# Two more token tiles taken from a transposed copy of the input, their statistics spread through DRAM, in a gated linear-attention kernel on one core

## The chip, the cores and the metric

One Trainium2 chip, one of its cores. The metric is the time of one execution in device microseconds; a kernel's time is the median of its runs. Engines are named as in the profile: PE is TensorE (PEld its weight loads), DVE is VectorE, ACT is ScalarE, POOL is GpSimd, SP is SyncE, which issues most of the DMAs here.

## The reference

Everything is float32, with 2048 tokens of 640 features, 32 heads of 20 and a hidden width of 1536. A layer norm without weights is followed by a linear attention with a learned softmax feature map and by an MLP that gates it:

```python
xn = (x - mean(x)) / sqrt(var(x) + 1e-5)
q, k, v = split(xn @ wqkv)                       # 32 heads of 20 each
phi = lambda t: concat(softmax(t @ w_phi), softmax(-t @ w_phi))   # per head, 20 -> 40
kv, z = phi(k).T @ v, sum(phi(k))                # over all tokens, per head
s = ((phi(q) @ kv) / (phi(q) . z + 1e-6)) @ wo
g = silu(gelu(xn @ w1 + b1) @ w2 + b2)
out = x + s * g
```

The host hands the kernel x twice, as it is and transposed (xt), and regroups the weights; it does no arithmetic.

## The kernel before

**Precision.** A float32 matmul is made of three passes in fp32r: every operand is kept as a high and a low part, a "split" of one ACT copy (the high part) and one DVE subtraction (the low part), and PASSES multiplies high by high, high by low and low by high.

**Stages.** Phase 1 handles 16 token tiles of 128 tokens: layer norm, transposition of x, projections to k, v and q, feature maps, and the sums kv and z. Then come twelve units of the MLP, with the queries' normalisation beside them, and the output. In the stages that matter here the order of every engine's queue is the order of the code; nothing is scheduled. Before phase 1 the key weights are folded with w_phi on PE (fold_w, L179, 24 + 6 matmuls of L174), and ahead of that PE runs ten matmuls of a constant (L521).

**How a tile is normed and transposed.** There are two ways.

- Tiles 0 to 5: norm (L255) takes the tile from x with tokens on partitions; DVE makes its statistics (L230 to L232), POOL a power of -0.5 (L233), and DVE or ACT norms the tile (L246, L252). transpose_x (L357) has five PE transposes (L363) into PSUM, pA, and plain (L282) splits from there: ACT at L285, DVE at L287.
- Tiles 6 to 15, as pairs q = t // 2: load_xr (L262) loads the pair's columns from xt into a slab xr, with features on partitions. pair_stats (L330) makes the statistics of each tile from x as above; at the second tile SP writes them to DRAM (L337) and reads them back to all 128 partitions (L339, tile bc). pair_sub (L343) subtracts the means on POOL (L346, two instructions), pair_mul (L349) multiplies by the reciprocal deviations on DVE (L351), and pair_plain (L353) splits from xr.

plain writes to xp and, for odd tiles, also to a slab b that two pairs share (beside, L276). Every project of tile t reads them.

**The loop over tiles (L577 to L606)**, for t = 2 to 5. PE runs project(t, wk), for t = 3 and 5 kv_pair(t - 3), and value(t), in whose middle a lambda may put transpose_x(t + 2); for t = 4 and 5 fold_pair(t - 4) follows (two groups of L174, read by ACT at L196 and L199 and by DVE at L197 and L198). On the other engines feat1 (L386) reads the projected keys: DVE takes a maximum (L389), a difference (L392) and a minimum (L395), and POOL the reversed half (L396); feat2 is an exponential on ACT (L405); key_fin sums heads on DVE (L413, L445) and scales on POOL (L418). spill (L294) writes a pair's split columns to DRAM.

**PSUM.** project, transpose_x, fold and the first matmuls take their accumulators from one pool of three slots (pA, two banks each) that are used in turn. The slot is free again when its readers are done: L392 for keys, ACT's L434 for values, L285 and L287 for a transposed tile, the last reading of fold_pair at L198.

**Rows and slabs.** Tiles of x, raw weights and bc come from a pool of 11 rows, xr, e and the split weights from one of 23 slabs, each in turn.

Of the kernel before, what the change touches and what calls it, by code (L numbers as in the profile page):

```python
# [46 lines left out]
def hedgehog_gated_mlp_kernel(ctx: ExitStack, tc: tile.TileContext, x, xt_in, wqk, bd, wv, wo, w1, b1, w2, b2, out_t):  # L47
# [33 lines left out]
    def slab(dt, name, shape=(P, 2, D)):  # L81
        return slabs.tile(list(shape), dt, tag="S", name=name)

    def row(shape, dt, name):
        return rows.tile(shape, dt, tag="R", name=name)

    def bankA():
        return pools["A"].tile([P, 2, 512], F32, tag="A", name="pA")
# [136 lines left out]
    def stats(t, sm, mean, rstd):  # L225
        xt = xts.pop(t)
        st = sm[:, :12]
        for i in range(2):
            with tc.issue_after(last_feat[0].ins) if last_feat[0] is not None and not by_hand[0] else ExitStack():
                nc.vector.bn_stats(st[:, 6 * i:6 * i + 6], xt[:, i * HALF:(i + 1) * HALF])  # L230
        nc.vector.bn_aggr(sm[:, 12:14], st.rearrange("p (a b) -> p a b", a=2))
        nc.vector.tensor_scalar(rstd, sm[:, 13:14], LN_EPS, None, op0=OP.add)  # L232
        nc.gpsimd.tensor_tensor(rstd, rstd, mhalf[:], op=OP.pow)  # L233
        if mean is not None:
            nc.vector.tensor_copy(mean, sm[:, 12:13])
        return xt
# [3 lines left out]
    def norm_a(t):  # L240
        sm = small.tile([P, 16], F32, tag="st", name="st")
        nrm[t] = sm, stats(t, sm, None, sm[:, 14:15])

    def norm_b(t):
        sm, xt = nrm.pop(t)
        nc.vector.tensor_scalar(xt[:], xt[:], sm[:, 12:13], sm[:, 14:15], op0=OP.subtract, op1=OP.mult)  # L246
        xns[t] = xt
# [7 lines left out]
    def norm(t):  # L255
        norm_a(t)
        norm_b(t)
# [4 lines left out]
    def load_xr(q):  # L262
        h, p = divmod(q, SLOTS)
        xr = slab(F32, "xr", (P, KC, W2))[:]
        src = xt_in.rearrange("(k p) (h o q t) -> p k h o q t", p=P, h=NH, o=2, q=SLOTS)[:, :, h, :, p]
        nc.sync.dma_start(xr[:, :, :P], src[:, :, 0])
        nc.sync.dma_start(xr[:, :, P:], src[:, :, 1])
        xrs[q] = xr
# [13 lines left out]
    def plain(q, o, v):  # L282
        parts = [(xp[:, 0:5, :, at(q)], v)] if o == 0 else [(beside(q), v[:, 0:2]), (xp[:, 5:8, :, at(q)], v[:, 2:5])]
        for dst, src in parts:
            nc.scalar.activation(dst[:, :, 0, :], src, AF.Copy)  # L285
        for dst, src in parts:
            nc.vector.tensor_tensor(dst[:, :, 1, :], src, dst[:, :, 0, :].bitcast(F32), op=OP.subtract)  # L287

    def stat_x(q, o, k, a):
        if o == 0:  # L290
            return xp[:, k, a, at(q)]
        return beside(q)[:, k, a, :] if k < 2 else xp[:, k + 3, a, at(q)]
# [37 lines left out]
    def pair_stats(t):  # L330
        if t % 2 == 0:
            pst[0] = small.tile([P, 2, 2], F32, tag="pst", name="pst")
        sm = small.tile([P, 16], F32, tag="st", name="st")
        stats(t, sm, pst[0][:, t % 2, 0:1], pst[0][:, t % 2, 1:2])
        if t % 2:
            q = t // 2
            nc.sync.dma_start(st_dram[q].rearrange("i p s -> p i s"), pst[0][:])  # L337
            bc = row([P, W2, 2], F32, "bc")
            nc.sync.dma_start(bc[:].rearrange("p t s -> p (t s)"),  # L339
                              st_dram[q].rearrange("i p s -> (i p s)").partition_broadcast(P))  # L340
            pld[q] = bc

    def pair_sub(q):  # L343
        bc, xr = pld[q], xrs[q]
        for o in (slice(0, P), slice(P, W2)):
            nc.gpsimd.tensor_tensor(xr[:, :, o], xr[:, :, o], bc[:, None, o, 0].to_broadcast([P, KC, P]),  # L346
                                    op=OP.subtract)

    def pair_mul(q):  # L349
        bc, xr = pld.pop(q), xrs[q]  # L350
        nc.vector.tensor_tensor(xr, xr, bc[:, None, :, 1].to_broadcast([P, KC, W2]), op=OP.mult)  # L351

    def pair_plain(q):  # L353
        for o in range(2):
            plain(q, o, xrs[q][:, :, o * P:(o + 1) * P])

    def transpose_x(t):  # L357
        q, o = divmod(t, 2)
        xn = xns.pop(t)
        ps = bankA()  # L360
        flat = ps[:].rearrange("p a b -> p (a b)")
        for k in range(KC):
            nc.tensor.transpose(flat[:, k * P:(k + 1) * P], xn[:, k * P:(k + 1) * P], ident[:])  # L363
        plain(q, o, flat[:, :D].rearrange("p (k t) -> p k t", t=P))
# [3 lines left out]
    def project(t, ws, mid=None, at_k=3):  # L368
        q, o = divmod(t, 2)
        ps = bankA()  # L370
        n = 0
        for k in range(KC):
            if k == at_k and mid is not None:
                mid()
            for a, b in PASSES:
                for hf in range(2):
                    nc.tensor.matmul(ps[:, hf, :HALF], stat_x(q, o, k, a),  # L377
                                     ws[k][:, b, hf * HALF:(hf + 1) * HALF],
                                     start=n == 0, stop=n == 3 * KC - 1)
                n += 1  # L380
        return ps

    def heads(ps):
        return ps[:, :, :HALF].rearrange("p a (h d) -> p a h d", d=DH)

    def feat1(ps, later=None):  # L386
        p4 = heads(ps)
        mx = small.tile([P, 2, 16], F32, tag="mx", name="mx")
        nc.vector.tensor_reduce(mx[:], p4, axis=AX.X, op=OP.max)  # L389
        e = slab(F32, "e")[:]  # L390
        e5 = e.rearrange("p a (h s d) -> p a h s d", s=2, d=DH)
        nc.vector.tensor_tensor(e5[:, :, :, 0, :], p4, mx[:, :, :, None].to_broadcast([P, 2, 16, DH]),  # L392
                                op=OP.subtract)
        nr = small.tile([P, 2, 16], F32, tag="nr", name="nr")
        last_feat[0] = nc.vector.tensor_reduce(nr[:], e5[:, :, :, 0, :], axis=AX.X, op=OP.min)  # L395
        rest = lambda: nc.gpsimd.tensor_tensor(e5[:, :, :, 1, :], nr[:, :, :, None].to_broadcast([P, 2, 16, DH]),  # L396
                                               e5[:, :, :, 0, :], op=OP.subtract)
        if later is None:
            rest()
        else:  # L400
            later.append(rest)
        return e.rearrange("p a b -> p (a b)")
# [28 lines left out]
    def value(t, mid=None):  # L431
        ps = project(t, wv_s, mid)
        v, v3 = value_row()
        nc.scalar.activation(v3[:, :, :DH].rearrange("p (a h) d -> p a h d", a=2), heads(ps), AF.Copy)  # L434
        return v
# [12 lines left out]
    def key_fin(ef):  # L448
        scale_heads(ef, key_sums(ef))
        return ef  # L450
# [10 lines left out]
    vs, es, phis, xns, wk_s, wq_s = {}, {}, {}, {}, [], [None] * 4  # L461
# [54 lines left out]
    phase1 = ExitStack()  # L516
    phase1.enter_context(tc.manual_schedule(engines={mybir.EngineType.PE, mybir.EngineType.SP}))
    one = nc.const_aps.tensor(1.0, [P, P], F32)
    for pw in (bankA(),):
        for i in range(10):  # L520
            nc.tensor.matmul(pw[:, 0, :P], one, one, start=True, stop=True)  # L521
    startup = ExitStack()
    startup.enter_context(tc.manual_schedule())
# [35 lines left out]
    es[0] = feat1(pk)  # L559
    split_v(3)  # L560
    pk = project(1, wk_s, lambda: transpose_x(2))
    load_xr(3)
    x_in(8)
    x_in(9)
# [2 lines left out]
    feat2(es[0])  # L567
    norm(3)
    es[1] = feat1(pk)
    vs[0] = value(0)  # L570
    phis[0] = key_fin(es.pop(0))
    feat2(es[1])
    vs[1] = value(1, lambda: transpose_x(3))
    norm(4)
    phis[1] = key_fin(es.pop(1))
    vf = [v_forms(0), v_forms(1)]
    for t in range(2, 6):  # L577
        pk = project(t, wk_s)
        if t % 2:
            kv_pair(t - 3)  # L580
        es[t] = feat1(pk)
        if t == 4:
            next(vf[0])
        if t == 2:
            norm(5)
        if t == 3:
            pair_stats(6)
            pair_stats(7)
        if t > 3:
            pair_stats(t + 4)  # L590
        if t in (3, 4, 5):
            spill(t - 3)
        if t == 5:
            x_in(10)
        if t == 4:
            pair_sub(3)
            pair_mul(3)
        vs[t] = value(t, (lambda: transpose_x(t + 2)) if t < 4 else None)
        if t >= 4:
            fold_pair(t - 4)  # L600
        if t == 5:
            next(vf[0])
        feat2(es[t])
        if t == 4:
            pair_plain(3)
        phis[t] = key_fin(es.pop(t))  # L606
# [179 lines left out]
    for p in range(5, 8):  # L786
        t = 2 * p
# [18 lines left out]
        def rest(t=t, p=p):  # L806
            if p == 5:
                next(vb)
                next(vb, None)
            later.pop(0)()  # L810
            feat2(es[t])
            if p == 6:
                t_sums(7)
            if p == 7:
                next(qf)
# [542 lines left out]
```

## Time and profile before

| | us |
|---|---|
| median of 3 runs | 652.42 |
| the three runs | 652.40, 652.42, 653.68 |
| the profiled execution | 653.69 |
| its span, first to last instruction | 652.0 |
| PE busy | 646.4 (99%) |
| DVE busy | 486.9 (75%) |
| POOL busy | 400.7 (61%) |
| ACT busy | 237.9 (36%) |

A row of the time line begins with the start in us from the span's start and a duration in us, followed by engine, line, operation, output <- input, shapes and the number of instructions that were merged; in brackets stand the idle time before it and what ended that. A float32 matmul that isn't fp32r shows as two instructions. A row of the windows names a stretch, its length, the busy time and number of instructions of PE, PEld, DVE, ACT and POOL, the granted clock of PE, the share of the DMA engines and GB/s. A row of the waits says who waited at which line for whom: us in total, times, longest.

### The profile page before, as it was taken

What the parts mean: (1) busy time and instruction counts of PE and PEld (TensorE: products, weight loads), DVE (VectorE), ACT (ScalarE), POOL (GpSimd) and SP (SyncE); (2) the same over time, 40 slices, a digit from 0 to 9 for tenths busy, and PEclk for the clock granted to TensorE, in tenths of its full rate; (3) what the DMA queues carried; (4) which work ended last, traced back from release to release, by engine and by line L of the source; (5) the groups of instructions that cost most, each with busy time, mean ns of one, the idle gap of its engine ahead of it and who ended that gap; (6) DMA issues with size and microseconds to landing.
All of it is one profiled execution on the core that took longest, in us unless ns stands there. A gap on an engine that the chain in (4) does not pass through costs nothing. (4 is left out here: it accounts for less than half of the span.)

```text
span 652.0 us, 11424 instructions
## 1 busy us (share of the span) xinstructions
PE 646.4 (99%) x4396; PEld 561.4 (86%) x4396; DVE 486.9 (75%) x734; ACT 237.9 (36%) x345; POOL 400.7 (61%) x371
## 2 busy tenths in 40 slices
PE   9999999999999999999999999999999999999997
PEld 9999999999999998888888888888888886766866
DVE  5785976789887777587978977858889899853232
ACT  3522422334343348144343355742231524032130
POOL 2656466897967765857878775355462966343321
PEclk9999999999999999999999999999999999999999
DMA  9705377495312486355987998695969499999942
GB/s 349 281 2 146 116 279 219 102 308 150 124 42 62 143 280 245 121 188 183 306 236 258 244 414 286 123 336 195 177 232 249 65 269 206 317 266 260 301 135 80
DMA packets 164447, 135.15 MB, mean 207 GB/s; under 512 B 89394, under 2 KB 128562, under 8 KB 164010
## 3 DMA queue, kind: packets, MB, share of 16 engines
q1 hardware_dynamic: 161658, 122.84, 64.2%
q10 hardware_dynamic: 2736, 11.60, 4.8%
q8 instruction: 34, 0.56, 0.4%
q14 instruction: 19, 0.16, 0.1%
HBM read 86.03 MB, written 48.38 MB: 206 GB/s over the span
## 5 line engine op out<-in xcount | busy, mean ns | idle before, releaser
L944 PE MATMUL pB<-hs,w2s 128*128 128x512 f32 x720 | 165.8, 389 | 0.0
L944 PEld LDWEIGHTS pB<-hs,w2s 128*128 128x128 f32 x720 | 135.0, 188 | 28.8 <-DVE y L953 0.8
L915 PE MATMUL pB<-xp,w1s 128*128 128x512 f32 x324 | 81.3, 389 | 0.0
L915 PE MATMUL pB<-xd,w1s 128*128 128x512 f32 x324 | 79.3, 389 | 0.0
L1102 PE MATMUL pB<-oT,wo 128*128 128x512 f32 (+1 forms) x315 | 72.3, 381 | 0.0
L418 POOL TENSOR_TENSOR eq<-eq,rc 128x1280 f32<-128x1280 f32 x16 | 37.9, 2369 | 55.0 <-DVE rc L1006 36.7
L915 PEld LDWEIGHTS pB<-xd,w1s 128*128 128x128 f32 x324 | 60.8, 188 | 12.6
L915 PEld LDWEIGHTS pB<-xp,w1s 128*128 128x128 f32 x324 | 60.8, 188 | 12.6
L1102 PEld LDWEIGHTS pB<-oT,wo 128*128 128x128 f32 x315 | 57.2, 188 | 13.8 <-PE pB L1049 2.5
L953 DVE TENSOR_TENSOR y<-pB,y 128x512 f32<-128x512 f32 x100 | 63.1, 676 | 1.4 <-PE pB L944 1.4
L920 ACT ACTIVATE pB<-pB,b1t 128x512 f32<-128x512 f32 x48 | 31.8, 662 | 79.0 <-DVE pB L1183 29.2
L405 ACT ACTIVATE e<-e 128x1280 f32<-128x1280 f32 x32 | 40.7, 1273 | 53.0 <-POOL e L396 49.2
L377 PE MATMUL pA<-wk,xp 128*128 128x320 f32 x384 | 59.6, 310 | 0.0
L396 POOL TENSOR_TENSOR e<-nr,e 128x640 f32<-128x640 f32 x32 | 43.5, 1361 | 24.1 <-DVE nr L395 24.0
L377 PEld LDWEIGHTS pA<-wk,xp 128*128 128x128 f32 x384 | 56.9, 188 | 0.1
L418 POOL TENSOR_TENSOR e<-e,rc 128x1280 f32<-128x1280 f32 x16 | 37.8, 2368 | 24.0 <-DVE rc L445 24.0
L993 POOL TENSOR_TENSOR ez<-eq,zrep 128x1280 f32<-128x1280 f32 x16 | 47.3, 2957 | 2.6 <-DMA eq<-e_dram 2.6
L485 POOL TENSOR_TENSOR w1s<-raw,w1s 128x640 fp32r<-128x640 f32 (+1 forms) x18 | 27.3, 1517 | 28.9 <-ACT w1s L484 28.9
L377 PE MATMUL pA<-wv,xp 128*128 128x320 f32 x240 | 37.7, 311 | 0.0
L149 POOL TENSOR_TENSOR w2s<-raw,w2s 128x640 fp32r<-128x640 f32 x23 | 36.0, 1588 | 0.2 <-ACT w2s L147 0.2
L1105 POOL TENSOR_TENSOR xres<-gt,xres 128x256 f32<-128x256 f32 x20 | 14.3, 736 | 35.3 <-DVE gt L1104 35.3
L377 PEld LDWEIGHTS pA<-wv,xp 128*128 128x128 f32 x240 | 35.5, 188 | 0.1
(182 smaller groups left out, 1139.7 us busy)
## 6 DMA issues: line engine op xcount, KB each, us to landing
raw<-in_w_dram SPq DMA_DIRECT2D x42, 320.0 KB
e_dram<-e ACTq DMA_DIRECT2D x16, 640.0 KB
eq<-e_dram SPq DMA_DIRECT2D x16, 640.0 KB
phi_t<-eq SPq DMA_DIRECT2D x64, 160.0 KB
phT<-phi_t SPq DMA_DIRECT2D x20, 480.0 KB
xt<-in_x_dram SPq DMA_DIRECT2D x16, 320.0 KB
xres<-in_xt_dram SPq DMA_DIRECT2D x20, 256.0 KB
out_dram<-xres SPq DMA_DIRECT2D x18, 256.0 KB
```

The lines of the kernel that those rows point to most:

```text
L149: eng.tensor_tensor(sl[:, 1, :], raw, sl[:, 0, :].bitcast(F32), op=OP.subtract)
L377: nc.tensor.matmul(ps[:, hf, :HALF], stat_x(q, o, k, a), ws[k][:, b, hf * HALF:(hf + 1) * HALF], start=n == 0, stop=n == 3 * KC - 1)
L396: rest = lambda: nc.gpsimd.tensor_tensor(e5[:, :, :, 1, :], nr[:, :, :, None].to_broadcast([P, 2, 16, DH]), e5[:, :, :, 0, :], op=OP.subtract)
L405: nc.scalar.activation(ef, ef, AF.Exp)
L418: nc.gpsimd.tensor_tensor(e3, e3, rc[:, :, None].to_broadcast([P, 64, DH]), op=OP.mult)
L485: nc.gpsimd.tensor_tensor(sl[:, 1, :n], src, sl[:, 0, :n].bitcast(F32), op=OP.subtract)
L915: nc.tensor.matmul(bank[ch][:], tl[:, a, off + wo_:off + wo_ + P], mov(blk, b), start=new and n == 0, stop=n == len(mms) - 1, skip_group_c ...
L920: nc.scalar.activation(ps, ps, AF.Gelu_apprx_tanh, bias=b1t[:, f:f + 1])
L944: nc.tensor.matmul(ps[:], ws[i][:, b, d * P:(d + 1) * P], hs[o][i][:, a, :], start=i == n == 0, stop=(i, n) == (GF - 1, 2), skip_group_che ...
L953: nc.vector.tensor_tensor(y, ps[:], y, op=OP.add)
L993: nc.gpsimd.tensor_tensor(zv, ef, zf, op=OP.mult)
L1102: nc.tensor.matmul(ps[:, mv], w, o[:, mv], start=n == 0, stop=n == 15, skip_group_check=True)
```

## The change

Tiles 4 and 5 change from the first way to the second. load_xr(2) is added ahead of load_xr(3). norm(4), norm(5), transpose_x(4) and transpose_x(5) go; pair_stats(4) and pair_stats(5) stand behind feat1(1) and value(0), pair_sub(2) and pair_mul(2) take norm(5)'s place at t = 2, and pair_plain(2) stands at t = 3 ahead of pair_stats(6). The ten constant matmuls in one slot become nine in three.

```diff
-    for pw in (bankA(),):
-        for i in range(10):
+    for pw in (bankA(), bankA(), bankA()):
+        for i in range(3):
             nc.tensor.matmul(pw[:, 0, :P], one, one, start=True, stop=True)
...
     pk = project(1, wk_s, lambda: transpose_x(2))
+    load_xr(2)
     load_xr(3)
...
     es[1] = feat1(pk)
+    pair_stats(4)
     vs[0] = value(0)
+    pair_stats(5)
     phis[0] = key_fin(es.pop(0))
     feat2(es[1])
     vs[1] = value(1, lambda: transpose_x(3))
-    norm(4)
     phis[1] = key_fin(es.pop(1))
...
         if t == 2:
-            norm(5)
+            pair_sub(2)
+            pair_mul(2)
         if t == 3:
+            pair_plain(2)
             pair_stats(6)
             pair_stats(7)
...
-        vs[t] = value(t, (lambda: transpose_x(t + 2)) if t < 4 else None)
+        vs[t] = value(t, (lambda: transpose_x(t + 2)) if t < 2 else None)
```

The lines of the changed kernel are four higher behind the added ones. Three places of the engines' queues follow. The first is PE's, from the end of project(2) to the start of project(3), with value(2) between them; before:

```order
L377 MATMUL pA<-wk_250,xp 128x320 x6
L377 MATMUL pA<-wv,xp 128x320 x18
L363 MATMUL pA<-ident,xt 128x128 x5
L377 MATMUL pA<-wv,xp 128x320 x12
L377 MATMUL pA<-wk_195,b_296 128x320 x6
```

Now, over the same place and the first rows of project(3):

```order
L377 MATMUL pA<-wk_251,xp 128x320 x6
L377 MATMUL pA<-wv,xp 128x320 x30
L377 MATMUL pA<-wk_196,b_297 128x320 x6
L377 MATMUL pA<-wk_207,b_297 128x320 x6
L377 MATMUL pA<-wk_217,xp 128x320 x6
```

The five transposes are gone from the middle of value(2), and so are those of value(3) (not shown). The second place is DVE's, from feat1(2) (its last two instructions) to the split of tile 5; before:

```order
L392 TENSOR_TENSOR e<-pA,mx 128x32x20
L395 TENSOR_REDUCE nr<-e 128x32
L230 BN_STATS st<-xt 128x6 x2
L231 BN_AGGR st<-st 128x2
L232 TENSOR_SCALAR st<-st 128x1
L246 TENSOR_SCALAR xt<-xt,st 128x640
L287 TENSOR_TENSOR xp<-pA,xp 128x5x128
L413 TENSOR_REDUCE rc<-e 128x64
L445 RECIPROCAL rc<-rc 128x64
L389 TENSOR_REDUCE mx<-pA 128x32
L392 TENSOR_TENSOR e<-pA,mx 128x32x20
L395 TENSOR_REDUCE nr<-e 128x32
```

Behind that came the statistics of tiles 6 and 7 and then the split of tile 5 from pA. Now, from the end of feat1(2) to the first statistics of tile 6:

```order
L395 TENSOR_REDUCE nr<-e 128x32
L351 TENSOR_TENSOR xr<-xr,bc 128x1280
L413 TENSOR_REDUCE rc<-e 128x64
L445 RECIPROCAL rc<-rc 128x64
L389 TENSOR_REDUCE mx<-pA 128x32
L392 TENSOR_TENSOR e<-pA,mx 128x32x20
L395 TENSOR_REDUCE nr<-e 128x32
L287 TENSOR_TENSOR xp<-xr,xp 128x5x128
L287 TENSOR_TENSOR b_688<-xr,b_688 128x2x128
L287 TENSOR_TENSOR xp<-xr,xp 128x3x128
L230 BN_STATS st<-xt 128x6 x2
```

The product of the pair stands where statistics and norm of tile 5 stood, and the splits of tiles 4 and 5, now from xr, stand ahead of the statistics of tiles 6 and 7 and behind feat1(3). The third place is SP's, from the loads of xr to the first spill; before:

```order
L266 DMA xr<-in_xt_dram 128x5x128
L267 DMA xr<-in_xt_dram 128x5x128
L142 DMA xt<-in_x_dram 128x640 x2
L266 DMA xr<-in_xt_dram 128x5x128
L267 DMA xr<-in_xt_dram 128x5x128
L337 DMA st_dram<-pst 128x2x2
L339 DMA bc<-st_dram 128x512
L295 DMA xp_dram<-xp 128x16x128
```

Now:

```order
L266 DMA xr<-in_xt_dram 128x5x128
L267 DMA xr<-in_xt_dram 128x5x128
L266 DMA xr<-in_xt_dram 128x5x128
L267 DMA xr<-in_xt_dram 128x5x128
L142 DMA xt<-in_x_dram 128x640 x2
L266 DMA xr<-in_xt_dram 128x5x128
L267 DMA xr<-in_xt_dram 128x5x128
L337 DMA st_dram<-pst 128x2x2
L339 DMA bc<-st_dram 128x512
L337 DMA st_dram<-pst 128x2x2
L339 DMA bc<-st_dram 128x512
L295 DMA xp_dram<-xp 128x16x128
```

One pair of loads and one round of statistics through DRAM have been put in; the round of tiles 4 and 5 stands first, that of tiles 6 and 7 behind it.

## The prediction

> **What bounds the kernel now.** I read the engine table of the page first, then the windows of the stage that the change touches, then the waits of TensorE (PE).
>
> ```profile
> PE 646.4 (99%) x4396; PEld 561.4 (86%) x4396; DVE 486.9 (75%) x734; ACT 237.9 (36%) x345; POOL 400.7 (61%) x371
> ...
> 33.00:95.00 62.00, 62.00 (x677) 61.51 (x676) 47.77 (x82) 17.43 (x25) 35.41 (x39) 1.00 0.43 135
> ...
> PE pA L521 <- PEq L1348: 0.8, 1, 0.8
> ```
>
> PE is busy for 646.4 of 652.0 us; between 33 and 95 us it is busy all the time (its column is the second: 62.00 of 62.00), and in the first 100 us it waits once, for the program's start. So the kernel is as long as PE's queue, and an edit counts in two ways only: in the matmuls it takes from that queue, and in the waits it puts into it. DVE, ACT and POOL have room on average, which says nothing about one stretch of some 30 us.
>
> **What it removes from PE.** The ten transposes of tiles 4 and 5 stood inside value(2) and value(3) (L598).
>
> ```profile
> 37.35 2.80 PE L377 MATMUL pA<-wv,xp 128*128 128x320 f32 x18
> ...
> 42.29 1.92 PE L377 MATMUL pA<-wk,b 128*128 128x320 f32 x12
> ...
> 48.11 2.02 PE L377 MATMUL pA<-wv,b 128*128 128x320 f32 x12
> ...
> 53.15 4.56 PE L377 MATMUL pA<-wk,xp 128*128 128x320 f32 x30
> 57.55 4.56 PE L377 MATMUL pA<-wv,xp 128*128 128x320 f32 x30
> 61.95 2.83 PE L174 MATMUL pA<-folds 120*128 120x120 f32 x24
> ...
> 70.44 2.02 PE L377 MATMUL pA<-wv,b 128*128 128x320 f32 x12
> ...
> 74.94 2.83 PE L174 MATMUL pA<-folds 120*128 120x120 f32 x24
> ```
>
> Value(2) takes 42.29 - 37.35 = 4.94 us from its start to the next project; value(4), without transposes, 61.95 - 57.55 = 4.40. Value(3) takes 53.15 - 48.11 = 5.04, and value(5) 74.94 - 70.44 = 4.50. That is 0.54 twice: **-1.08 us**.
>
> The warm-up has nine matmuls (two passes each) in place of ten.
>
> ```profile
> 0.84 4.60 PE L521 MATMUL pA<-const-float32-1.0 128*128 128x128 f32 x20 [0.84 <-PEq L1348]
> ...
> 4.06 0.91 DVE L541 TENSOR_TENSOR folds<-folds 120x720 f32<-120x720 f32 x1 [4.06 <-DMA folds<-in_bd_dram]
> ...
> 5.03 6.40 PEld L174 LDWEIGHTS pA<-folds 120*128 120x128 f32 x48
> 5.24 6.38 PE L174 MATMUL pA<-folds 120*128 120x120 f32 x48
> ```
>
> One matmul is (5.24 - 0.84) / 10 = 0.44 us, but the first fold also needs DVE's block mask, ready at 4.06 + 0.91 = 4.97, and its weight load started at 5.03. What is late next is thus DVE: **-0.03 us**, and PE then stands idle for about 0.4 us ahead of the fold. The three banks cost nothing, by the code: the two allocations more at the start stand against two transposes less, so that from tile 4 on each matmul group meets the bank that it met before. PE's gain is 1.11 us, if nothing else comes to bind.
>
> **What it adds, and to whom.** Tiles 4 and 5 now go the way of tiles 6 and 7: statistics, out to DRAM, back to all partitions, a subtraction on POOL, a product on DVE, a split from SBUF. PE's first use of tile 4 is in project(4), at 53.15 - 1.11 = 52.0. I follow the chain from project(2), whose end (37.35) moves by 0.03 only. The steps' sizes come from these rows:
>
> ```profile
> 29.04 0.82 DVE L395 TENSOR_REDUCE nr<-e 128x32 f32<-128x640 f32 x1
> ...
> 49.35 0.88 DVE L230 BATCH_NORM_STATS2 st<-xt 128x6 f32<-128x320 f32 x2
> ...
> 51.85 0.14 DVE L235 COPY pst<-st 128x1 f32<-128x1 f32 x1
> ...
> 57.75 0.82 DVE L389 TENSOR_REDUCE mx<-pA 128x32 f32<-128x640 f32 x1 [0.43 <-PE pA L377]
> ...
> 60.21 0.88 DVE L230 BATCH_NORM_STATS2 st<-xt 128x6 f32<-128x320 f32 x2
> ...
> 65.25 1.49 DVE L351 TENSOR_TENSOR xr<-xr,bc 128x1280 f32<-128x1280 f32 x1 [3.67 <-POOL xr L346]
> ...
> 69.17 0.49 DVE L198 TENSOR_TENSOR sr<-sr,pA 128x320 f32<-128x320 f32 x1
> ...
> 71.63 1.48 DVE L413 TENSOR_REDUCE rc<-e 128x64 f32<-128x1280 f32 x1
> ...
> 73.62 0.76 DVE L389 TENSOR_REDUCE mx<-pA 128x32 f32<-128x640 f32 x1
> ```
>
> ```profile
> 60.37 1.27 POOL L396 TENSOR_TENSOR e<-nr,e 128x640 f32<-128x640 f32 x1 [0.18 <-DVE nr L395]
> ...
> 62.12 3.10 POOL L346 TENSOR_TENSOR xr<-xr,bc 128x640 f32<-128x640 f32 x2
> ```
>
> feat1 holds DVE for 60.21 - 57.75 = 2.46 and starts 0.2 behind project's end (57.75 against PE's next start, 57.55); POOL's reversal starts 60.37 - 57.75 = 2.62 behind it and takes 1.27. Statistics of two tiles are 51.85 + 0.14 - 49.35 = 2.64 on DVE, head sums with reciprocal 73.62 - 71.63 = 1.99.
>
> The first round is hidden. After feat1(1) (29.8) DVE does the statistics of 4 and 5 (2.64), two head sums (3.98) and a split of under 1 us, and is free by 37.4, as project(2) ends. Then: feat1(2) at 37.5, POOL's reversal 40.1 to 41.4, pair_sub(2) to 44.5 (3.10), pair_mul(2) to 46.0 (1.49), head sums to 48.0, feat1(3) to 50.4, and only then the split of tiles 4 and 5. The trip of their statistics starts near 33 and takes 7.5 (below), so bc(2) is there at about 40.5, ahead of pair_sub(2). DVE stands still from 40.0 to 44.5 at pair_mul(2), where it did statistics and a norm before; behind it wait those head sums, feat1(3), the split and the statistics of 6 and 7. Tile 4's first piece is split by about 51.2 to 52.4; project(4) needs it from 52.6 on (the fifth matmul). Narrow, but hidden.
>
> The split's last pieces, however, fall beside POOL's reversal of tile 3. This order of DVE and POOL stands in the trace once already, for a later tile:
>
> ```profile
> 182.22 0.82 DVE L287 TENSOR_TENSOR xp<-xr,xp 128x640 fp32r<-128x640 f32 x1
> 182.96 1.50 DVE L287 TENSOR_TENSOR b<-xr,b 128x256 fp32r<-128x256 f32 x1
> ...
> 184.85 0.81 DVE L389 TENSOR_REDUCE mx<-pA 128x32 f32<-128x640 f32 x1
> ...
> 182.45 1.73 POOL L396 TENSOR_TENSOR e<-nr,e 128x640 f32<-128x640 f32 x1 [3.94 <-DVE nr L395]
> ...
> L287 DVE TENSOR_TENSOR b<-xr,b x5: 417/418/1503, 70.8 to 183.0; 128x256 fp32r<-128x256 f32 x5
> L287 DVE TENSOR_TENSOR b<-pA,b x3: 425/425/425, 18.7 to 52.4; 128x256 fp32r<-128x256 f32 x3
> ```
>
> The split from xr took 184.85 - 182.22 = 2.63 us there, because its middle piece took 1503 ns in place of 418 while POOL's took 1.73 us in place of 1.27; from pA it took 425 each time. Bounds: 2.63 with the collision, 2.63 - 1.08 = 1.55 without. I take 2.63, as engines and order are the same.
>
> The Trainium skill, page "SBUF — State Buffer", section "Who interferes with whom", says this in general: a VectorE instruction with both inputs in SBUF and a GpSimd instruction that reads SBUF lock each other out, and one with an input in PSUM doesn't. The rows above agree (1503 against 425), and the rule speaks against this change, which moves the split's source from PSUM to SBUF; without it the sum below would end 1.08 lower.
>
> The second round isn't hidden. Statistics of tiles 6 and 7 now start at 50.4 + 2.63 = 53.0, where they started at 49.35. From there the trip through DRAM runs as before:
>
> ```profile
> 52.59 0.37 SPq L337 DMA_DIRECT2D st_dram<-pst  x1
> 55.94 0.34 SPq L339 DMA_DIRECT2D bc<-st_dram  x1
> ...
> 77.98 0.37 SPq L337 DMA_DIRECT2D st_dram<-pst  x1
> 82.09 0.32 SPq L339 DMA_DIRECT2D bc<-st_dram  x1
> ...
> SPq L339 <- DMA st_dram<-pst: 11.9, 3, 5.4
> ...
> 57.00:58.00 1.00, 1.00 (x9) 1.00 (x9) 0.57 (x2) 0.00 (x0) 0.18 (x1) 1.00 1.22 33
> 58.00:59.00 1.00, 1.00 (x9) 1.00 (x8) 0.97 (x2) 0.00 (x0) 1.00 (x1) 1.00 0.59 135
> 59.00:60.00 1.00, 1.00 (x9) 1.00 (x8) 0.96 (x2) 0.00 (x0) 1.00 (x1) 1.00 1.02 284
> ```
>
> L337 was issued 52.59 - 49.35 = 3.24 behind the first statistics, so now at 56.25. SP then waits for it: 3.35 to L339 the first time, 4.11 the second, up to 5.8 in the longest of three (5.4 of waiting and the issue's 0.37). I take 3.35, the same pair of tiles with as little ahead of it in SP's queue: L339 at 59.6. How long its 256 KB take has no row. By the last column (GB/s, so KB in each window of 1 us) 168 KB had moved by 59.0 and 452 by 60.0, the next transfer's among them, so not under 3.4; and POOL read the result at 62.12 without waiting, so not over 6.2. I take 4.1, near the lower end: bc lands at 63.7. POOL would have been ready at 53.0 + 2.64 + 1.99 + 2.62 + (62.12 - 60.37) = 62.0. So **pair_sub(3) waits 1.7 us for the DMA**, runs until 66.8 and releases pair_mul(3) at 66.83, in place of 65.25: 1.58 later.
>
> Behind pair_mul(3) on DVE's queue stand the readings of fold_pair(0). Three slots rotate (fold, fold, project(5), and value(5) in the first fold's again), and the third L198 frees that slot: 69.17 + 0.49 - 65.25 = 4.41 behind pair_mul, so at 71.24, and PE starts at 71.29. PE itself would be there at 70.44 - 1.11 = 69.33. It **waits 1.96 us**, and the balance is -1.11 + 1.96 = **+0.85 us**. Before, the bank was free at 69.66, 0.78 ahead of PE; that cover is what goes. Next is the second fold of fold_pair(1), in project(5)'s slot: feat1(5) has read it 1.7 us behind its start, at 73.62 + 1.58 + 1.7 = 76.9, and PE comes at 74.94 + 0.85 + 1.4 = 77.2. The loads of xr(2), 2 x 320 KB ahead of xr(3) in SP's queue, delay those behind them by 2.3 us at the 284 GB/s of the last window; their reader comes at 41. From there on PE is dense again and carries the 0.85 to the end.
>
> The profiled execution took 653.69 us around its span of 652.0; the median of three was 652.42. The sum is a difference, so I put it on the median: **653.3 us**. About 0.2% (1.3 us) is what a measurement of this kernel can tell from no change.
>
> **The rivals.**
>
> *The trip hides.* If bc(3) is there by 61.9, pair_mul(3) comes at 65.0, the bank is free at 69.45 and nearly the whole gain stays: -1.0, 651.4. It takes 1.8 us off the chain: no collision (1.08) and a second leg of 3.4 (0.7). The collision at 182 speaks against it. Either alone gives -0.2 or +0.15, still no measurable change.
>
> The Trainium skill, page "DMA: Bandwidth & Descriptors", section "Anatomy of one DMA — SWDGE (gpsimd) path", fits 2.0 us and bytes / 436 GB/s to each DMA: as an estimate 4.6 us for both legs where I take 7.45, by which this rival would be the outcome even with the collision (bc at 60.9, POOL ready at 62.0). Its fit is for GpSimd's queue; SP's row disagrees, with 3.35 us for 2 KB.
>
> *The store's leg is long, the slower side.* Of three such stores one kept SP for 5.8 us. With that leg in place of 3.35 the bank is free 2.4 later and the balance is +3.3, 655.7. It decides from legs of 7.9 together, where the balance passes +1.3; the store of 4.11 would give +1.6. For it: two of the three would do. Against it: the one at this very place didn't.
>
> *The clock comes late.* The warm-up's passes come every 0.22 us, those of the later folds every 2.83 / 24 = 0.12, and the first 48 took 6.38 us, 0.7 above that: the early ones ran slow. An idle gap of 0.4 us ahead of the fold could put the faster rate off; all 48 slow would be 10.6, so between 0 and +4.2. That it has to do with the gap, no row shows.
>
> *It doesn't do what it says.* The matmuls are gone from PE's queue by its order, so only a wait could take their place; that is the forecast.
>
> **How the numbers follow.** Forecast (value(5) waits; -0.2 to +1.3): 48%. Trip hidden (-0.2 to -1.1): 14%. Long legs (+1.3 to +3.3): 25%. Late clock (over +1.3): 8%. It does something else: 5%. PE's gain can't pass 1.11 us, so faster by over 0.2% is left to the measurement's own scatter, 4%; slower holds the long legs, the clock and some of the rest, 35%; the same 61%. The range goes from the whole gain, 651.4, to 655.0, short of the longest leg's 655.7.
>
> **What would show it.** PE with no L363 inside value(2) and value(3), and value(5) about 0.85 late with a wait of 2 us for DVE's L198 ahead of it; POOL's pair_sub(3) waiting for DMA bc; DVE's split of tile 5 at 1.5 us beside POOL's 1.7; L337 of tiles 6 and 7 near 56. I am wrong if PE doesn't wait there, if it waits ahead of project(4), or if the second store isn't the one that lands late.

## The result, and the profile after

The changed kernel takes 653.79 us (median of 14 runs, 652.9 to 654.81) where the kernel before takes 652.76 us (14 runs, 652.22 to 653.73). The ratio is 1.0016, with a 95% interval of 1.0009 to 1.0024: about 1.0 us slower, and under the 1.3 us (0.2%) that the prediction takes for a measurable change. The profiled execution is the slowest of the 14, 654.81 us around a span of 653.1.

TensorE's (PE) timeline of the changed kernel, from value(2) to the fold behind value(5); columns are start, length, engine, line, operation, and in brackets the idle time ahead with what ended it:

```profile
36.96 4.56 PE L377 MATMUL pA<-wv,xp 128*128 128x320 f32 x30
41.36 1.92 PE L377 MATMUL pA<-wk,b 128*128 128x320 f32 x12
...
47.17 2.02 PE L377 MATMUL pA<-wv,b 128*128 128x320 f32 x12
49.03 2.80 PE L377 MATMUL pA<-wv,xp 128*128 128x320 f32 x18
51.67 4.56 PE L377 MATMUL pA<-wk,xp 128*128 128x320 f32 x30
...
67.64 1.39 PE L457 MATMUL kv<-e,v 128*32 128x40 f32 x128
70.99 3.27 PE L377 MATMUL pA<-wv,b 128*128 128x320 f32 x12 [1.96 <-ACT xp L285]
74.06 3.10 PE L377 MATMUL pA<-wv,xp 128*128 128x320 f32 x18
77.00 2.83 PE L174 MATMUL pA<-folds 120*128 120x120 f32 x24
```

Value(2) now takes 41.36 - 36.96 = 4.40 us and value(3) 51.67 - 47.17 = 4.50: 0.54 less each, with no transposes inside. Project(4) follows without a gap. Ahead of value(5) PE stands idle for 1.96 us. The row names ACT's L285 as releaser, but that copy writes tile 6's part of xp and nothing for value(5); the matmul waits for the readers of its bank, and DVE's third L198 ends just then. PE starts 0.63 us behind that L198's start (70.36). In the two runs with a wait alone below, ACT's copy had ended at 69.0 and 69.1 us, and PE still started 0.64 and 0.63 us behind the same L198, at 74.34 and 72.32. The chain behind it, on DVE, POOL and SyncE's queue (SPq):

```profile
49.98 0.89 DVE L287 TENSOR_TENSOR xp<-xr,xp 128x640 fp32r<-128x640 f32 x1
50.79 1.49 DVE L287 TENSOR_TENSOR b<-xr,b 128x256 fp32r<-128x256 f32 x1
52.20 0.55 DVE L287 TENSOR_TENSOR xp<-xr,xp 128x384 fp32r<-128x384 f32 x1
52.67 0.87 DVE L230 BATCH_NORM_STATS2 st<-xt 128x6 f32<-128x320 f32 x2
...
66.44 1.49 DVE L351 TENSOR_TENSOR xr<-xr,bc 128x1280 f32<-128x1280 f32 x1 [5.46 <-POOL xr L346]
...
70.36 0.49 DVE L198 TENSOR_TENSOR sr<-sr,pA 128x320 f32<-128x320 f32 x1
```

```profile
50.14 1.86 POOL L396 TENSOR_TENSOR e<-nr,e 128x640 f32<-128x640 f32 x1
...
61.01 0.55 POOL L233 TENSOR_TENSOR pst<-pst,mhalf 128x1 f32<-128x1 f32 x1
63.26 3.15 POOL L346 TENSOR_TENSOR xr<-xr,bc 128x640 f32<-128x640 f32 x2 [1.70 <-DMA bc<-st_dram]
```

```profile
55.92 0.36 SPq L337 DMA_DIRECT2D st_dram<-pst  x1
59.17 0.33 SPq L339 DMA_DIRECT2D bc<-st_dram  x1
```

Read it from left to right in time: the split's middle piece takes 1.49 us beside POOL's L396 (1.86), the statistics of tile 6 start at 52.67, the store goes out at 55.92, the broadcast at 59.17, pair_sub(3) starts at 63.26 after 1.70 us of waiting for it, pair_mul(3) at 66.44, and the bank is free at 70.36 + 0.49 = 70.85.

One thing stands in no step of the prediction. Value(5)'s 30 matmuls, 4.50 us before, take 77.00 - 70.99 = 6.01 here. The windows of this stretch say why, three of the changed kernel and, last, the middle one in the kernel before; the columns are the window, its length, the busy time of PE, its weight loads, DVE, ACT and POOL, then the granted clock:

```profile
67.80:71.30 3.50, 1.54 (x130) 1.45 (x123) 3.40 (x8) 2.60 (x5) 0.00 (x0) 1.00 1.14 345
71.30:74.71 3.41, 3.41 (x15) 3.41 (x14) 3.38 (x6) 0.34 (x1) 0.00 (x0) 0.50 0.64 237
74.71:78.20 3.49, 3.49 (x28) 3.49 (x27) 3.39 (x7) 0.71 (x1) 3.17 (x2) 1.00 0.02 5
...
71.30:74.71 3.41, 3.41 (x25) 3.41 (x25) 3.34 (x5) 0.00 (x0) 0.86 (x1) 1.00 0.28 104
```

For 3.41 us behind the wait the clock was at half, and in that window 15 matmuls went through where 25 did before. That is 1.5 us at this place. Three of the 14 executions have a mean clock of 0.996 as this one does (654.81, 654.47, 654.58); the other eleven have 0.999 or 1.000 and a median of 653.75. So the median's 1.0 us isn't the clock's.

### The profile page after: what moved, and what is told of

It is laid out like the page before. It is cut to its first block, busy times and chain, and to the rows that moved or that the text cites. A ratio compares the mean times of both kernels' runs of the same rounds, so it can differ in the third digit from the quotient of the medians.

```text
span 653.1 us, 11407 instructions
## 1 busy us (share of the span) xinstructions
PE 646.2 (99%) x4384; PEld 561.3 (86%) x4384; DVE 484.5 (74%) x735; ACT 237.8 (36%) x345; POOL 405.8 (62%) x373
## 4 chain that ended last, share of the span: by engine, by line
PE 81%; DVE 7%; POOL 5%; DMA 3%; issue 2%; ACT 1%; ACTq 0%; SPq 0%; POOLq 0%; DVEq 0%
PE pB L948 24%; PE pB L919 22%; PE pB L1106 11%; PE pA L377 9%; PE pA L684 6%; PE pB L1053 2%; PE pA L174 2%; DMA st_dram<-pst 1%; PE qV L684 1%; POOL xr L346 1%; DVE xr L351 1%; POOL xr L300 1%; POOL e L396 1%; POOL xd L324 1%; PE qY L684 1%
## 5 line engine op out<-in xcount | busy, mean ns | idle before, releaser
L418 POOL TENSOR_TENSOR eq<-eq,rc 128x1280 f32<-128x1280 f32 x16 | 37.9, 2371 | 54.0 <-DVE rc L1010 36.0
L377 PE MATMUL pA<-wk,xp 128*128 128x320 f32 x384 | 59.6, 310 | 0.0
L396 POOL TENSOR_TENSOR e<-nr,e 128x640 f32<-128x640 f32 x32 | 44.8, 1399 | 20.9 <-DVE nr L395 20.9
L418 POOL TENSOR_TENSOR e<-e,rc 128x1280 f32<-128x1280 f32 x16 | 39.1, 2447 | 19.6 <-DVE rc L445 19.6
L149 POOL TENSOR_TENSOR w2s<-raw,w2s 128x640 fp32r<-128x640 f32 x23 | 36.0, 1585 | 0.2 <-ACT w2s L147 0.2
```

The lines of the kernel that those rows point to most:

```text
L149: eng.tensor_tensor(sl[:, 1, :], raw, sl[:, 0, :].bitcast(F32), op=OP.subtract)
L377: nc.tensor.matmul(ps[:, hf, :HALF], stat_x(q, o, k, a), ws[k][:, b, hf * HALF:(hf + 1) * HALF], start=n == 0, stop=n == 3 * KC - 1)
L418: nc.gpsimd.tensor_tensor(e3, e3, rc[:, :, None].to_broadcast([P, 64, DH]), op=OP.mult)
```

## The experiments

Theory A is the prediction's: two times 0.54 us go, the warm-up is worth next to nothing, the banks stay as they were, and the late second trip of statistics makes value(5) wait 2.0 us for its bank. The rivals are in each expectation. Every run was compared with the kernel before on the same chip.

**The warm-up edit alone** (on the kernel before):

```diff
-    for pw in (bankA(),):
-        for i in range(10):
+    for pw in (bankA(), bankA(), bankA()):
+        for i in range(3):
```

> The kernel before with the warm-up edit alone (nine matmuls in three banks). Theory A, the prediction's: DVE's block mask is next behind the warm-up, so 0.03 to 0.34 us go (0.34 is what the profiled execution after showed at the first fold), 652.4 to 652.7 us against 652.76, no wait at value(5). Rival C, the extra time comes from the start, because the shorter warm-up brings the full clock later: 653.5 us or more, with the first 48 folds longer than 6.4 us.

Measured: 654.05 us against 652.91, ratio 1.0016 (1.0007 to 1.0024). By its time rival C was right, and by its place not. The first 48 folds took 6.48 us, over its 6.4, but they began at 4.99, and the transposes behind them came at 11.31, against 11.45 before: nothing was lost there. The extra lies at 242 us. PE's timeline there:

```profile
240.54 0.60 PE L680 MATMUL pA<-wq,xp 128*128 128x320 f32 x3
242.22 1.62 PE L915 MATMUL pB<-xp,w1s 128*128 128x512 f32 x6 [1.07 <-DVE e L392]
```

At 242 us one stage's PSUM pool closes and the next one opens over the same banks (L1126). With two more allocations at the start, the new stage's first bank falls on one that the features of a late tile still read, as the wait for DVE's L392 shows. So my expectation of "no more than the warm-up" was wrong for this edit alone. Two runs separate the parts.

**Nine warm-up matmuls in the one bank** (on the kernel before):

```diff
-        for i in range(10):
+        for i in range(9):
```

> The kernel before with nine warm-up matmuls in its one bank, so without the two more bank allocations. Theory A, the prediction's, the shorter warm-up is worth 0.03 to 0.34 us and the 1.1 us of the run with three banks come from the banks' rotation (PE's wait at 242 us for DVE's L392): 652.5 to 652.9 us against 652.9, no wait at the first L915. Rival C, the shorter warm-up itself costs 1.1 us: 654.0 us.

Measured: 652.98 us against 652.77, ratio 1.0004 (0.9995 to 1.0013), and no wait at the first L915. The shorter warm-up is worth nothing that can be measured; the 1.1 us were the banks.

**The tiles with the old number of warm-up matmuls** (on the changed kernel):

```diff
-    for pw in (bankA(), bankA(), bankA()):
-        for i in range(3):
+    for pw, n in ((bankA(), 4), (bankA(), 3), (bankA(), 3)):
+        for i in range(n):
```

> The changed kernel with ten warm-up matmuls (4, 3, 3 in the three banks) in place of nine. Theory A: the tiles' part is -1.08 + 1.96 = +0.88 us and nothing of the start changes: 653.6 to 654.1 us against 652.76, PE's wait ahead of value(5) stays at 1.9 to 2.3 us. Rival C: with the old warm-up the loss is gone, 652.8 us or less.

Measured: 653.91 us against 652.91, ratio 1.0016 (1.0007 to 1.0025). Its value(5):

```profile
70.55 2.00 PE L377 MATMUL pA<-wv,b 128*128 128x320 f32 x12 [1.68 <-ACT xp L285]
```

The wait is 1.68 us, a little under the range, and the 12 matmuls behind it run at their usual speed. The loss is that of the tiles, as theory A has it; rival C is out. This trace also shows where the 1.0 us of the median lies. PE's time at the start differs from trace to trace with the moment at which the clock comes up (7.04 us before, 5.88 here), so I count from the first transposes behind the folds, 11.45 before and 10.90 here. To the fold behind value(5) it is 63.49 before and 75.03 - 10.90 = 64.13 here, 0.64 more: the wait less the transposes. About 0.3 more comes behind it: the kv sums that start at 161.68 here start at 160.83 in the run with nine warm-up matmuls in one bank (transposes at 11.01), 0.96 apart by the same count. A wait of 0.25 us of PE's weight loads for ACT's L434, at 152.62, is part of it; no run shows why it is there.

**The tiles with one bank at the start** (on the changed kernel):

```diff
-    for pw in (bankA(), bankA(), bankA()):
-        for i in range(3):
+    for pw in (bankA(),):
+        for i in range(9):
```

> The changed kernel with its nine warm-up matmuls in one bank. Theory A, the two allocations more at the start keep every later tile in the PSUM bank that it had before: without them the first bank of the next stage, at 242.8 us, falls on the bank that the last features read, whose L392 ends at 246.8 in the changed kernel's trace, so PE waits 4.1 us there: 657.9 us. Rival E, the banks don't matter where the tiles don't come by PE: 653.8 us.

Measured: 660.07 us against 652.77, ratio 1.0105 (1.0089 to 1.0121). The wait is there and as long as expected, but the time is 2.2 us above 657.9. PE in this kernel:

```profile
241.66 0.60 PE L684 MATMUL pA<-wq,xp 128*128 128x320 f32 x3
246.32 2.90 PE L919 MATMUL pB<-xp,w1s 128*128 128x512 f32 x6 [4.05 <-DVE e L392]
```

Six matmuls of a kind that took 1.55 us before take 2.90: the clock record is at half from 244.52 to 251.34, so PE worked 5.0 us at half speed behind the wait, which costs 2.5 us in this execution (660.79). So the three banks of the change earn nothing by themselves: they pay for the two allocations that went with the transposes. Rival E is out.

**The statistics ahead of tile 5's split** (on the changed kernel), which takes the collision and that split off the chain:

```diff
-            pair_plain(2)
+            plain(2, 0, xrs[2][:, :, :P])
             pair_stats(6)
             pair_stats(7)
+            plain(2, 1, xrs[2][:, :, P:])
```

> The changed kernel with the statistics of tiles 6 and 7 put between the split of tile 4 and that of tile 5, so that they start 1.8 us earlier on DVE (50.9 in place of 52.7) and don't stand behind the piece that collides with POOL. Theory A, the chain DVE's statistics, trip through DRAM, POOL's subtraction, DVE's product, bank: the broadcast lands at 61.5, POOL is ready at 61.6, pair_sub(3) starts at 61.6 in place of 63.3, and PE waits 0.0 to 0.4 us ahead of value(5) in place of 2.0: 651.7 to 652.1 us against 652.76 before, 1.7 to 2.1 less than the changed kernel, and no slow stretch of the clock. Rival B, the bank's last reader is ACT's copy for the spill or another step that doesn't hang on the statistics: the wait stays near 2 us, 653.8 us.

Measured: 652.00 us against 652.91, ratio 0.9984 (0.9975 to 0.9993), 1.8 us less than the changed kernel. Its PE and POOL:

```profile
67.32 1.40 PE L457 MATMUL kv<-e,v 128*32 128x40 f32 x128
68.89 1.99 PE L377 MATMUL pA<-wv,b 128*128 128x320 f32 x12 [0.17 <-ACT xp L285]
```

```profile
61.20 3.11 POOL L346 TENSOR_TENSOR xr<-xr,bc 128x640 f32<-128x640 f32 x2 [0.84 <-DMA bc<-st_dram]
```

The wait is down to 0.17 us. One move on DVE took away the whole loss, through store, broadcast, POOL and DVE's product: rival B is out. POOL still waits 0.84 us for the broadcast, where I had expected both at 61.6: the broadcast came at 61.2, POOL was free at 60.4. The same middle piece of the split, for tile 5 and with POOL elsewhere, takes 0.42 us in place of 1.49, behind statistics that now start at 50.45:

```profile
50.45 0.87 DVE L230 BATCH_NORM_STATS2 st<-xt 128x6 f32<-128x320 f32 x2
...
53.01 0.42 DVE L287 TENSOR_TENSOR b<-xr,b 128x256 fp32r<-128x256 f32 x1
```

**The statistics in DVE's idle time**, with the nine warm-up matmuls in two banks (on the changed kernel):

```diff
-    for pw in (bankA(), bankA(), bankA()):
-        for i in range(3):
+    for pw, n in ((bankA(), 5), (bankA(), 4)):
+        for i in range(n):
...
             pair_sub(2)
+            pair_stats(6)
+            pair_stats(7)
             pair_mul(2)
...
             pair_plain(2)
-            pair_stats(6)
-            pair_stats(7)
```

> The changed kernel with the statistics of tiles 6 and 7 on DVE between pair_sub(2) and pair_mul(2), where DVE stood still from 40 to 44 us, and the nine warm-up matmuls in two banks (5 and 4), which keeps the bank at 242 us free. Theory A: the trip through DRAM is over by 53, pair_sub(3) waits for POOL alone (61.6), no wait ahead of value(5) but up to 0.2 us: the whole gain of 1.1 us, 651.6 to 652.0 us. Rival F, DVE's earlier statistics come into POOL's way (pair_sub(2)) or delay tile 4's split so that project(4) waits: 652.5 us or more, with a PE wait at 44 to 53 us.

Measured: 651.40 us (11 runs, 650.98 to 652.0) against 652.77, ratio 0.9978 (0.9969 to 0.9987). It beats both kernels, by 1.4 us the one before. Its trip through DRAM, POOL's subtraction and PE:

```profile
45.78 0.36 SPq L337 DMA_DIRECT2D st_dram<-pst  x1
...
48.82 0.33 SPq L339 DMA_DIRECT2D bc<-st_dram  x1
```

```profile
59.76 0.55 POOL L233 TENSOR_TENSOR pst<-pst,mhalf 128x1 f32<-128x1 f32 x1
60.28 3.10 POOL L346 TENSOR_TENSOR xr<-xr,bc 128x640 f32<-128x640 f32 x2
```

```profile
67.28 1.40 PE L457 MATMUL kv<-e,v 128*32 128x40 f32 x128
68.61 2.03 PE L377 MATMUL pA<-wv,b 128*128 128x320 f32 x12
70.47 2.80 PE L377 MATMUL pA<-wv,xp 128*128 128x320 f32 x18
73.11 2.83 PE L174 MATMUL pA<-folds 120*128 120x120 f32 x24
```

The store goes out 10 us earlier, POOL starts pair_sub(3) with no wait as soon as its own work is done, and PE has no gap. Rival F is out. The same tiles by the same way give the gain that the transposes promised, once their trip stands early enough. One thing doesn't fit: with one allocation more at the start than before and two transposes less, this run makes three allocations fewer than the warm-up edit alone, a full turn of the three slots. By turns alone it would meet the same bank at 242 us, yet it has no wait there. So the number of allocations doesn't settle which bank that is, and no run shows what does.

**A wait alone** (on the kernel before; the differences write what the next operation overwrites):

```diff
+        for _ in range(10 if i == 0 else 0):
+            dve(a[:, :HALF], b[:, HALF:], b[:, HALF:], OP.subtract)
         dve(a[:, :HALF], b[:, HALF:], pa[:, 0, :HALF], OP.subtract)
```

> The kernel before with ten more DVE differences of 128x320 (their result is overwritten) ahead of the third L198 of fold_pair(0), so that value(5)'s bank comes late with nothing else changed: ten by about 0.5 us less the cover of 0.78 makes PE wait 4.0 to 4.4 us there. Theory A, a wait there is passed on whole and the slow clock comes of the idle time: 652.9 + 4.2 = 657.1 us where the clock stays full, 658.8 us where it falls to half for 3.4 us (that costs 1.7 us), and it falls more often than in the changed kernel's 3 of 14 executions. Rival D, the slow stretch has nothing to do with the idle time: 657.1 us throughout. Rival G, later slack takes the wait up again: under 656.5 us.

Measured: 659.59 us against 652.77, ratio 1.0104 (1.0089 to 1.0118), all four runs at a mean clock of 0.993 or 0.994. PE, and the windows of the stretch:

```profile
68.39 1.39 PE L459 MATMUL kv<-e,v 128*32 128x40 f32 x128
74.34 3.54 PE L379 MATMUL pA<-wv,b 128*128 128x320 f32 x12 [4.55 <-DVE sr L198]
77.68 3.45 PE L379 MATMUL pA<-wv,xp 128*128 128x320 f32 x18
80.97 2.83 PE L174 MATMUL pA<-folds 120*128 120x120 f32 x24
```

```profile
69.00:72.30 3.30, 0.79 (x85) 0.66 (x71) 3.10 (x7) 0.73 (x3) 0.00 (x0) 1.00 0.00 0
72.30:75.71 3.41, 1.37 (x5) 1.40 (x6) 3.27 (x8) 0.00 (x0) 0.00 (x0) 0.50 0.20 79
75.71:79.13 3.42, 3.42 (x15) 3.42 (x14) 3.35 (x6) 0.00 (x0) 0.75 (x1) 0.50 0.31 118
79.13:82.50 3.37, 3.37 (x28) 3.37 (x27) 2.68 (x7) 0.70 (x1) 3.37 (x5) 1.00 0.00 0
```

Here the releaser is named as DVE's L198. The wait came out at 4.55 us, and value(5) takes 80.97 - 74.34 = 6.63 in place of 4.50: 4.55 + 2.1 = 6.7 us, against 6.8 measured. The wait is passed on whole (rival G is out), and the slow clock comes with it in every execution (rival D is out). I had reckoned with one slowed window; there were two.

**A shorter wait alone**, six differences in place of ten:

> The kernel before with six DVE differences in place of ten: 6 x 0.52 = 3.1 us less the cover of 0.78 makes PE wait 2.2 to 2.5 us ahead of value(5), nearly the changed kernel's 2.0, without the changed tiles. Theory A: 652.85 + 2.35 = 655.2 us with the full clock, up to 1.7 more where a window of 3.41 us with the idle time in it is slowed (in the ten-difference kernel two windows, 6.83 us), which some and not all executions show: the windows lie at multiples of 3.41 us from the moment at which the clock came up. So the profiled execution's record falls, if at all, at such a multiple. Rival G, later slack takes the wait up: under 654.5 us.

Measured: 656.30 us against 652.87, ratio 1.0048 (1.0036 to 1.0061); four of the five runs have a mean clock of 0.996 or 0.997 and take 656.27 to 656.49 us; the fifth, at 0.998, takes 655.31, the wait alone. PE, and the windows:

```profile
72.32 3.08 PE L379 MATMUL pA<-wv,b 128*128 128x320 f32 x12 [2.44 <-DVE sr L198]
75.19 3.30 PE L379 MATMUL pA<-wv,xp 128*128 128x320 f32 x18
```

```profile
69.46:72.87 3.41, 0.97 (x48) 0.87 (x36) 3.21 (x8) 0.36 (x1) 0.00 (x0) 1.00 0.00 0
72.87:76.28 3.41, 3.41 (x15) 3.41 (x15) 3.38 (x6) 0.00 (x0) 0.00 (x0) 0.50 0.51 196
```

2.44 us of waiting and about 1.0 for the clock make the 3.4 of the median. At value(5) itself the clock costs more in the profiled execution: value(5) takes 78.33 - 72.32 = 6.01 us, 1.5 over its 4.50. Some of it is taken up behind, so there is a little of rival G's slack: of two waits of 0.2 us that the kernel before has in its queries' stage (PE's L680 for ACT's qx and DVE's v), neither is listed here, nor for the changed kernel. Rival G's forecast, under 654.5 us, is out. The profiled execution's clock came up at 4.60 and fell at 72.87, 68.27 us or 20.0 times 3.413 later, as expected.

**Matmuls in the idle time** (on the changed kernel), in three forms: eight behind the kv sums, eight ahead of them, four behind them. Those of the first have start=True, by which the kv bank also loses what it had summed up; the other two add.

```diff
+        if t == 5:
+            for i in range(8):
+                nc.tensor.matmul(kvp[0][:, 384:], one, one, start=True, stop=True, skip_group_check=True)
         vs[t] = value(t, (lambda: transpose_x(t + 2)) if t < 2 else None)
```

> The changed kernel with eight matmuls of 128x128 constants, into columns of the kv bank that nobody reads, ahead of value(5), where PE stands idle for 2.0 us (8 x 2 passes x 0.11 us = 1.8 us). Theory A, the wait is the loss and the slow clock behind it comes of the idle time: value(5) starts as late as in the changed kernel, no execution shows a mean clock of 0.996, its 12 first matmuls take 1.9 us in each, and the median is 653.3 to 653.8 us (the changed kernel's fast-clock executions are at 653.3 to 653.9). Rival D, the slow stretch has another cause (all engines' load at that time): it stays in some of the executions.

> The changed kernel with eight matmuls of constants (16 passes of 0.12 us, 1.9 us, added onto columns of the kv bank that nobody reads) ahead of the kv sums in front of value(5), so that PE has no idle time there. Theory A, the clock falls for idle time: value(5) starts at 70.6 to 71.0 as in the changed kernel, no clock of 0.996 in any execution, the median 653.2 to 653.8 us. Theory H, the hole of 1.7 us that the fillers behind the kv sums left in value(5) is a matter of how fast PE gets instructions behind many short ones: here the fillers stand ahead of the 128 short kv matmuls, so as in the changed kernel no hole. Rival, the fillers themselves cost: 654.5 us or more, with a hole again.

> The changed kernel with four such matmuls (8 passes, 0.9 us) between the kv sums and value(5). Theory A: value(5) starts at 70.6 to 71.0, about 1 us of idle time stays, no clock of 0.996: 653.2 to 653.8 us. Theory H, instructions come too slowly behind many short ones: half as many fillers leave a hole of at most 0.9 us in value(5), or none, since 1 us of idle time lets them catch up. Rival: the hole stays at 1.7 us and the median at 655 us, then it is something else that hangs on value(5).

Measured: 654.96 us (ratio 1.0031, 1.002 to 1.0041), 654.81 (1.0032, 1.0019 to 1.0044) and 653.66 (1.0013, 1.0004 to 1.0022). No execution of the three, 7, 5 and 11, has a mean clock under 0.999, which agrees with theory A on the clock; but eleven executions of the run with ten warm-up matmuls had none either, so it is weak evidence beside the two runs with longer waits. The medians missed for the first two, by a hole inside value(5). PE in the first, and in the third:

```profile
68.78 2.05 PE L604 MATMUL kv<-const-float32-1.0 128*128 128x128 f32 x16
70.58 0.69 PE L377 MATMUL pA<-wv,b 128*128 128x320 f32 x3
73.00 1.47 PE L377 MATMUL pA<-wv,b 128*128 128x320 f32 x9 [1.74 <-issue]
```

```profile
68.74 1.16 PE L604 MATMUL kv<-const-float32-1.0 128*128 128x128 f32 x8
70.62 1.85 PE L377 MATMUL pA<-wv,b 128*128 128x320 f32 x11 [0.72 <-ACT xp L285]
72.95 0.31 PE L377 MATMUL pA<-wv,b 128*128 128x320 f32 x1 [0.47 <-issue]
```

"Issue" means that nothing in the profile was waited for. The hole stands behind the same number of passes each time: 16 + 3, 16 + 3 in the second form (1.26 us), and 8 + 11. Theory H in my form, that the fillers must stand behind the short kv matmuls, fell with the second form. That PE ran out of instructions at a fixed place of its program would fit; it isn't shown, and the cause stays open.

## Why the prediction was right, point by point

- *The forecast.* +0.85 us on the median, 653.3; measured +1.03, 653.79, inside the range. No measurable change had the highest chance, and came.
- *The transposes, -1.08.* Right: 4.40 and 4.50 us for the two values. That the gain is real shows in the run with the early statistics, with 1.4 us off the median (0.9 to 2.0 by its interval).
- *The warm-up, -0.03, and DVE as what is late next.* Nothing that can be measured, by the run with nine matmuls in one bank. DVE's mask is late next, as forecast: PE waits 0.46 us for L541 in the run with the statistics ahead of tile 5's split. The first fold started 0.34 us earlier in the changed kernel (4.90 against 5.24), but little of it is kept: the run with the old number of matmuls, its first fold at 5.24 too, had its first transposes at 10.90, the changed kernel at 11.06. In the former the clock came up at 5.88, in the latter at 6.44, and that moves these rows more than one matmul does.
- *The three banks, nothing.* Right for the change as a whole, shown from both sides: without the tiles the edit costs 1.1 us, and the tiles without it cost 6 us more. The reason given, that slots are met in turn, is not enough: the run with two banks breaks it.
- *The first round hidden.* Right: no gap ahead of project(4).
- *The collision, 2.63 us of split.* Right: 52.67 - 49.98 = 2.69, the middle piece 1.49 us beside POOL and 0.42 without. In the profile before, the same piece read from PSUM took 0.42 at 18.66 and at 33.20 us, both times beside an operation of POOL on SBUF (L149 and L418), so it is the move from PSUM to SBUF that lets POOL hold it up.
- *The trip.* Predicted 56.25, 59.6 and 63.7; measured 55.92, 59.17 and 63.26. The legs were taken at 3.35 and 4.1 and came out at 3.25 and 4.09. The rivals that hid the trip or made its store leg long didn't come; the first, which needed 1.8 us off the chain, came true as soon as the statistics were moved 2.2 us forward (50.45 against 52.67 for their start).
- *The bank, PE waiting 1.96 us.* The mechanism is right. The hundredth is luck: the wait is 1.96 in the profiled execution, 1.68 with ten warm-up matmuls and 1.84 with one bank. The bank came 0.4 us earlier than reckoned, and PE 0.3.
- *Missed: the clock behind the wait.* The rival of the late clock looked at the start only. A wait of 2 us can put PE at half clock for a window, 1.5 us, in 3 of 14 executions. It is too rare to move the median; with 0.5 us more of waiting, in the kernel before with six differences, it came in four of five and did.
- *PE dense behind value(5), carrying the 0.85 to the end.* Not quite: about 0.3 us came on top between 75 and 161 us in the run with ten warm-up matmuls, where the wait was 1.68. So the nearness of 0.85 to 1.03 is in part luck, a wait a little shorter and a later loss that was not forecast. The difference is within the interval of the measurement (0.6 to 1.6 us).

## What to carry to other kernels

When work moves off the bounding engine, follow the new path to the last buffer it holds up: here 1.1 us of transposes came off TensorE, and one DVE order that started a DRAM trip 3 us later (55.92 against 52.59) gave back about 2.0. Then look for idle time on the path's own engines ahead of that point, since moving the two statistics into it turned +1.0 us into -1.4. And look for waits far from the edit when it adds or removes tile allocations: two more or two fewer at the start brought a wait of 1 or 4 us to a stage that begins 240 us later.

## What the runs showed of the hardware that was not expected

The clock gate works in windows. From the moment the clock came up, it fell after 19.00, 20.00, 20.00 and 70.00 times 3.413 us (6.44 to 71.30 in the changed kernel, 4.03 to 72.30 and 4.60 to 72.87 in the two with a wait alone, 5.58 to 244.52 with one bank), and it came back at such a multiple behind a window in which PE was busy throughout. In the window before the fall PE was idle for 1.96 us of 3.41 in the changed kernel; in the run with ten warm-up matmuls, whose clock came up at 5.88, 1.68 us of idle time lay inside the window from 67.3 to 70.7 and left the clock up. The Trainium skill, page "TensorE: Matmul & The Clock Gate", section "The HAM clock gate (the "warmup" mystery)", gives a free-running window of 3413 ns, with which these rows agree. The same page, section "HAM oscillation — how this bites in real kernels", puts the limit at idle gaps over about 3.4 us; here 1.96 us in one window was enough, and the measurement decides.

A stage's first PSUM bank can change with the tiles allocated long before it, by more than their number: the warm-up alone and the run with two banks are a full turn apart, and only the first waits at 242 us. And matmuls put into idle time aren't free even where nothing waits for them: sixteen short passes left a hole of 1.3 to 1.7 us a few matmuls later, eight one of 0.5.
